# Loading q for the next two blocks in small pieces from two queues, and moving half of a block's inner sums behind a later product

## The chip, the cores and the metric

The kernel runs on one core of a Trainium2 chip. A core has five engines that work side by side: TensorE (PE in the profile, with its weight loads shown apart as PEld), VectorE (DVE), ScalarE (ACT), GpSimd (POOL) and SyncE (SP), which here only starts DMA transfers. TensorE writes to PSUM; VectorE and ScalarE read PSUM and free it for the next product. Each engine works through its own instructions in order. The metric is the device time of one execution in microseconds (us); lower is better.

## The reference

Inputs are q, k, v of shape (8, 8, 576, 64) (batch, heads, sequence, head size), a gain of 64, and three weight matrices. All is float32.

```python
kv  = einsum('bhsd,bhse->bhde', k, v)
out = einsum('bhsd,bhde->bhse', q, kv)
rms = sqrt(mean(out * out, axis=-1, keepdims=True) + 1e-06)
x   = (out / rms * g_norm).transpose(0, 2, 1, 3).reshape(4608, 512)
g   = x @ w_gate                       # 512 x 1536
silu = g / (1 + exp(-g))
result = (silu * (x @ w_val)) @ w_out  # 1536 x 512
```

## The kernel before

**Blocks.** The 4608 rows of x are worked on in nine blocks of 512 rows. Block n needs the products kv of the batches that its rows belong to, its q, and from these its x (class `Att`). Then the block goes through a feed-forward stage (class `Ffn`) of two halves: `up`, which makes h = silu(x w_gate) * (x w_val), and `down`, which multiplies h by w_out. Blocks 0, 1 and 2 run alone, blocks 3 to 8 in pairs (class `Pair`).

**Fast products.** The matrix products use a scheme of seven products in place of eight (P1 to P7), with sums of operands made beforehand and sums of results made afterwards. From block 2 on it is used twice, one level inside the other. The outer sums of x are made by `sums`, and the inner sums (four operations over 128 x 896 elements, lines 132 and 133) by `inner_sums`. The sums of results are additions on VectorE that read PSUM (`r<-b,r`, `r<-c,r`, `r<-a,r` on line 132), and copies on ScalarE (line 803). PSUM has three banks named b, two named c, one named a and two named m; a product can start only when its bank has been emptied.

**Block 2's up** (class `Inner`) has twelve units: three groups d, each with four sets g of outer products. A unit runs seven inner products. Its weights are not resident: 128 x 512 pieces ("leaves", `t<-w`, lines 922 and 925) stream from DRAM into a pool of nine tiles. `Stream.pump`, called after each product, issues the next load as soon as the tile nine places back is free; all these loads stand on SP's queue.

**Work placed between.** While block 2's up runs, the attention work of block 3 and part of block 4's is placed in it. `up` takes a table `fill`: the entry i runs when the i-th unit's products have been issued. `ahead` makes this table: visits that make kv on TensorE (line 344), loads of k and v (line 294), loads of q (line 312), the transposes of block 3's q on VectorE (line 360), q times kv (line 399), squares on ScalarE (line 412), the reciprocal root in nine small VectorE steps (lines 442 to 444), the scaling (line 134) and the turning of x (line 459). Steps on VectorE are put into a list `chores`, and one is taken from it behind each product.

**q.** For a block, q is loaded in two tiles (i = 0, 1) of 128 x 1024. `load_quarters` fills a tile with 16 transfers (24 to 40 KB each for blocks 3 and 4: 32 partitions, runs of 128 bytes), eight for each half. In `ahead` a call moves eight of them, all on SP's queue, at one place: entries 1, 2, 3 and 4 for block 3, entries 6, 7, 8 and 9 for block 4.

**The order.** A planner orders each engine's instructions by its own estimate of when each can run; the order in the program is a priority and not a command. `tc.issue_after(x)` makes instructions on x's engine come behind x. Every DMA transfer, from whichever queue, is given one of eight completion semaphores in turn, and it waits until the transfer eight places before it in the planner's order has landed.

**Down.** `Down` runs P1, P6, P5, P7, P2, P4, P3. Behind P1 come the next block's products of q and kv and the rest of its attention (`steps`). The `then` table of `down` lets the caller place more: for block 2, `{1: blocks[PAIRED].inner_sums}` places the four inner sums of block 3 behind P1.

Of the kernel before, what the change touches and what calls it, by code (L numbers as in the profile page):

```python
# [18 lines left out]
def kernel(  # L19
# [41 lines left out]
    nc = tc.nc  # L61
# [152 lines left out]
    class Att:  # L214
# [83 lines left out]

        def load_quarters(self, i, pairs=(0, 1)):


            if pairs[0] == 0:
                self.q.append(ld_pool.tile([P, LD], F32, name="ld")[:, 0 : 2 * BLK])
            to = self.q[i].rearrange("p (j g d) -> p j g d", j=2, d=P // 4)
            cut = 2 * self.n
            spans = [(self.n - 1, S - D * self.n, 0, cut), (self.n, 0, cut, BLK // 32)]
            for j in pairs:
                for r in range(4):
                    h, d = divmod(r, 2)
                    for b, s0, g0, g1 in spans:  # L310
                        if g1 > g0:
                            nc.sync.dma_start(
                                out=to[32 * r : 32 * (r + 1), j, g0:g1],
                                in_=q[b, 4 * i + 2 * j + h, s0 : s0 + 32 * (g1 - g0), 32 * d : 32 * (d + 1)].rearrange(
                                    "(g p) d -> p g d", p=32
                                ),
                            )

        def load_q(self, i):
            if self.quarters:  # L320
# [132 lines left out]
        def turn_x(self, i):  # L453
            xt = self.xts[:, i].rearrange("p t j u d -> p t j (u d)")
            for j in range(0, NS, 2):
                ps = m_psum.tile([P, 2, 2, P], F32, name="m")
                for e in range(2):
                    for t in range(2):
                        self.turned_x = nc.tensor.transpose(ps[:, e, t], xt[:, t, j + e], ident)
                self.copied = nc.scalar.activation(  # L460
                    out=self.x[:, 2 * i + j // 2], in_=ps.rearrange("p e t c -> p e (t c)"), func=ACT.Copy, scale=gain
                )
# [51 lines left out]
        def half(self, i, pools=None):  # L514
            self.product(i, pools)
            self.root(i)
            self.scale(i)
            self.halves.append(self.scaled)
# [553 lines left out]
    class Ffn:  # L1072
        def __init__(self, n, att):
            self.n, self.att = n, att
            self.h = h_alone if n < PAIRED else h_slots[(n - PAIRED) % 2]
            self.ps, self.leaf_room, self.ended, self.owed = {}, None, None, None

            self.making, self.later, self.latest = [], [], []
            self.chores = []
            self.visited = None  # L1080

        def store(self, o, t, columns=slice(None)):
# [17 lines left out]
        def up(self, fill):  # L1100

            self.s1 = s_pool.tile([P, NP, HB], F32, name="s1")
            units = []
            for d in range(NP // 2):
                if self.n < DEEP:
                    units += [Up(self, 2 * d), Up(self, 2 * d + 1)]
                else:
                    shared = {}
                    units += [Inner(self, d, g, shared) for g in range(4)]
            units[0].prepare()  # L1110
            last = None
            for i, this in enumerate(units):
                if i + 1 < len(units):
                    units[i + 1].prepare()
                for unit, p in this.sequence(last):
                    if unit:
                        visited, self.visited = self.visited, None
                        with tc.issue_after(visited.ins) if visited else ExitStack():
                            unit.multiply(p)
                        self.make(4)  # L1120
                        if self.chores:
                            self.chores.pop(0)()
                last = this
                fill.get(12 * (i + 1) // len(units), lambda: None)()
            self.down_ = Down(self)
            self.down_.turn_t(5)
            for unit, p in last.sequence(None):
                if unit is None:
                    last.multiply(p)
# [136 lines left out]

    def ahead(ffn, att, then):

        def visits():
            visit(ffn, att, (0, 1))  # L1270
            att.load_quarters(0, (0,))

        def second():
            att.load_quarters(0, (1,))
            then.load_kv(0)

        def turn():
            visit(ffn, then, (0,), True)
            then.load_kv(1)
            ffn.chores += [lambda i=i: att.turn_q(i) for i in range(2)]  # L1280

        def half(i):
            with tc.issue_after(ffn.multiplied.ins):
                att.heads(i, range(NS), (m_psum, m_psum))
            ffn.visited = att.multiplied
            ffn.chores += att.chores(i)
            then.load_quarters(i, (0,))

        def turn_x(i):
            with tc.issue_after(ffn.multiplied.ins):  # L1290
                att.turn_x(i)
            ffn.visited = att.turned_x
            if i == 1:
                ffn.chores += att.sum_steps()

        def last():
            visit(ffn, then, (1,), True)
            while owed_sends:
                owed_sends.pop(0)()

        att.homes = {
            "qt": h_alone[:, 8:12], "sq": span(0, 8).rearrange("p (f t) -> p f t", f=4),
            "xts": span(8, 8).rearrange("p (f t) -> p f t", f=4),
        }

        def again(i):
            then.load_quarters(i, (1,))

        return {
            1: visits, 2: second, 3: lambda: att.load_quarters(1, (0,)), 4: lambda: att.load_quarters(1, (1,)),  # L1310
            5: turn, 6: lambda: half(0), 7: lambda: again(0), 8: lambda: half(1),
            9: lambda: (turn_x(0), again(1)), 10: lambda: turn_x(1), 11: last,
        }

    for n in range(PAIRED):
        ffn = Ffn(n, blocks[n])
        nxt = blocks[n + 1]
        if n == 0:

            with tc.issue_after(squared.ins), tc.issue_after(scaled.ins):  # L1320
                weights(2)
            ffn.plain_up(0, (0,))
            copied = blocks[0].copied
            blocks[0].turn_x(1)
            for f in range(NF):
                with tc.issue_after(blocks[0].copied.ins if f else copied.ins):
                    weights(2 * (f + 2))
                ffn.plain_up(f) if f else ffn.plain_up(0, (1,))
            weights(len(pieces))
            pairs = wo.rearrange("p (j e) d -> p e j d", e=2)  # L1330
            t2(pairs[:, 0, :, HD:DM], pairs[:, 1, :, HD:DM], pairs[:, 0, :, 0:HD])
            nxt.room = xi_alone.rearrange("p a b c -> p (a b c)")

            with tc.issue_after(sent.ins):
                for i in range(2):
                    nxt.load_kv(i)
                for i in range(2):
                    nxt.load_q(i)
            ffn.plain_end()
            for g in range(2):  # L1340
                nxt.kv(g)
            nxt.turn()
        elif n == 1:

            def third():
                visit(ffn, nxt, (0,))
                nxt.load_kv(1)

            def two_thirds():
                visit(ffn, nxt, (1,))  # L1350
                for i in range(2):
                    nxt.load_q(i)

            ffn.up({4: third, 8: two_thirds})
            nxt.turn()
            blocks[PAIRED].load_kv(0)
        else:
            ffn.up(ahead(ffn, nxt, blocks[PAIRED + 1]))
            nxt = blocks[PAIRED + 1]
            nxt.turn()  # L1360
            for g in range(2):
                blocks[PAIRED + 2].load_kv(g)
        if n:
            ffn.down_.opens = n + 1
        ffn.down(nxt, {1: blocks[PAIRED].inner_sums} if n == 2 else {})
        if n == 1:
            blocks[PAIRED].load_kv(1)
        if n == 0:
            blocks[2].load_kv(0)

            with tc.issue_after(nxt.halves[0].ins):
                for j in range(NP // 2):
                    t2(wv[j][:, 0:2], wv[j][:, 2:4], wg[j][:, 0:2])
            with tc.issue_after(ffn.down_.s4.ins):
                for j in range(NP // 2, NP):
                    t2(wv[j][:, 0:2], wv[j][:, 2:4], wg[j][:, 0:2])
# [60 lines left out]
```

## Time and profile before

| | us |
|---|---|
| median of 7 runs (1031.59 to 1036.12) | 1033.76 |
| profiled execution | 1034.03 |
| its span, first to last instruction | 1032.3 |
| TensorE busy | 1000.4 (97%) |
| VectorE busy | 684.7 (66%) |
| GpSimd busy | 360.6 (35%) |
| ScalarE busy | 228.9 (22%) |
| block 2's up, TensorE's first to last product in it | 270.9 to 371.8 |
| mean granted TensorE clock | 0.993 |

In the profile a line such as `L132 DVE TENSOR_TENSOR r<-b,r` is the instruction's line in the kernel, its engine, its operation and its output and inputs by the program's names. In a timeline the first number is the start and the second the length of the merged group in microseconds, `xN` the number of instructions; in brackets at the end stands how long the engine stood idle before it and what it waited for. `SPq` rows are DMA transfers being issued by SP; the data lands some microseconds later. In tables of stretches each engine has its busy time and, in brackets, its instructions; behind them come the granted TensorE clock as a share of full speed, the mean busy share of the 16 DMA engines and GB/s.

### The profile page before, as it was taken

The page shows a single profiled execution, that of the slowest core. Times are in us where ns is not written, and L with a number is a line of the kernel's source. Part 1 is how long each engine was busy: PE and PEld are TensorE (multiplying, and loading weights), DVE is VectorE, ACT ScalarE, POOL GpSimd, SP SyncE. Part 2 cuts the span into 40 slices and gives each one's busy share as a digit, 9 for nine tenths or more (in the row PEclk, how much of TensorE's full clock was granted, in tenths as well). Part 3 has the DMA queues.
Part 4 walks back from the last instruction along what each step waited for, and adds up shares of the span by engine and source line. Part 5 has one row for each costly group of instructions (what it writes and reads, how often), then busy time and mean ns, then how long its engine had stood idle before and what let it go on. Part 6 is the DMA issues. An engine that isn't in the chain of part 4 may idle for free.

```text
span 1032.3 us, 17746 instructions
## 1 busy us (share of the span) xinstructions
PE 1000.4 (97%) x6774; PEld 844.2 (82%) x6774; DVE 684.7 (66%) x1166; ACT 228.9 (22%) x357; POOL 360.6 (35%) x283
## 2 busy tenths in 40 slices
PE   6999999999989799999999999999999999999998
PEld 4544688888988788888888888888888888888887
DVE  2998788888557884665667656566676566666211
ACT  2765112221211211112111211211212112121100
POOL 0000263534024631345555102465652025556600
PEclk9999999999989989999999999999999999999999
DMA  8689543768888846586742454667403545543011
GB/s 230 203 254 266 116 86 128 238 204 206 246 196 201 239 110 160 150 217 170 171 133 62 114 127 146 164 167 186 126 12 72 117 151 163 153 142 106 1 41 41
DMA packets 255637, 155.20 MB, mean 150 GB/s; under 512 B 141632, under 2 KB 234816, under 8 KB 255552
## 3 DMA queue, kind: packets, MB, share of 16 engines
q1 hardware_dynamic: 224832, 150.13, 53.1%
q10 hardware_dynamic: 30656, 3.94, 2.4%
q8 instruction: 54, 0.88, 0.4%
q14 instruction: 31, 0.25, 0.1%
q0 software_dynamic: 64, 0.00, 0.0%
HBM read 117.97 MB, written 28.70 MB: 142 GB/s over the span
## 4 chain that ended last, share of the span: by engine, by line
PE 71%; DMA 4%; SPq 1%; DVE 0%; issue 0%; ACT 0%; DVEq 0%; ACTq 0%
PE b L789 24%; PE b L621 16%; PE c L789 11%; PE c L621 8%; PE a L789 6%; PE a L621 4%; DMA t<-w 2%; PE m L399 1%; PE m L344 1%; DMA w<-arena 1%; DMA ld<-in_q_dram 1%; DMA ld<-in_v_dram 1%; DVE r L132 0%; SPq L294 0%; SPq L962 0%
## 5 line engine op out<-in xcount | busy, mean ns | idle before, releaser
L789 PE MATMUL b<-arena,t 128*128 128x256 f32 (+1 forms) x1248 | 281.6, 365 | 13.4 <-DVE r L132 8.0
L789 PEld LDWEIGHTS b<-arena,t 128*128 128x128 f32 x1248 | 222.6, 193 | 44.9 <-DVE r L132 12.0
L132 POOL TENSOR_TENSOR r<-r 128x256 f32<-128x256 f32 (+1 forms) x105 | 110.5, 1054 | 310.8 <-DMA t<-w 153.0
L132 DVE TENSOR_TENSOR r<-b,r 128x512 f32<-128x512 f32 (+1 forms) x273 | 162.3, 607 | 85.6 <-PE b L789 78.8
L132 DVE TENSOR_TENSOR r<-c,r 128x512 f32<-128x512 f32 (+1 forms) x179 | 109.2, 618 | 94.9 <-PE c L789 45.0
L789 PE MATMUL c<-arena,t 128*128 128x256 f32 (+1 forms) x624 | 140.5, 362 | 0.9 <-ACT r L803 0.7
L133 POOL TENSOR_TENSOR t<-wo 128x512 f32<-128x512 f32 x54 | 78.4, 1474 | 173.9 <-DVE wo L132 105.5
L132 DVE TENSOR_TENSOR r<-a,r 128x512 f32<-128x512 f32 (+1 forms) x99 | 62.5, 632 | 105.0 <-PE a L621 66.8
L134 POOL TENSOR_TENSOR arena<-r 128x1024 f32<-128x1024 f32 (+1 forms) x46 | 96.2, 2107 | 95.7 <-DVE r L132 78.7
L789 PEld LDWEIGHTS c<-arena,t 128*128 128x128 f32 x624 | 111.8, 192 | 14.5 <-ACT r L803 1.1
L133 DVE TENSOR_TENSOR arena<-arena 128x512 f32<-128x512 f32 (+3 forms) x101 | 102.5, 1027 | 19.1 <-PE b L621 11.9
L621 PE MATMUL b<-wo,arena 128*128 128x256 f32 x432 | 99.1, 382 | 0.8 <-POOL arena L134 0.8
L621 PE MATMUL b<-t,arena 128*128 128x256 f32 x432 | 96.3, 380 | 0.0
L621 PEld LDWEIGHTS b<-wo,arena 128*128 128x128 f32 x432 | 81.1, 190 | 13.3 <-DVE arena L134 1.3
L621 PEld LDWEIGHTS b<-t,arena 128*128 128x128 f32 x432 | 82.1, 190 | 11.4 <-issue 0.2
L803 ACT COPY r<-b 128x512 f32<-128x512 f32 x63 | 36.9, 585 | 222.2 <-PE b L789 211.0
L789 PE MATMUL a<-arena,t 128*128 128x256 f32 (+1 forms) x288 | 72.3, 369 | 0.0
L789 PEld LDWEIGHTS a<-arena,t 128*128 128x128 f32 x288 | 53.2, 193 | 6.4
L621 PE MATMUL a<-wo,arena 128*128 128x256 f32 x216 | 48.4, 379 | 0.0
L621 PE MATMUL c<-t,s 128*128 128x256 f32 x216 | 48.1, 379 | 0.0
L621 PE MATMUL c<-wo,arena 128*128 128x256 f32 x216 | 48.1, 379 | 0.0
L621 PEld LDWEIGHTS c<-wo,arena 128*128 128x128 f32 x216 | 41.1, 190 | 5.5
(118 smaller groups left out, 1116.9 us busy)
## 6 DMA issues: line engine op xcount, KB each, us to landing
t<-w SPq DMA_DIRECT2D x219, 256.0 KB, 3.3
t<-w SPq DMA_DIRECT2D x75, 128.0 KB, 3.5
out_dram<-r SPq DMA_DIRECT2D x17, 512.0 KB, 3.0
ld<-in_k_dram SPq DMA_DIRECT2D x26, 288.0 KB, 5.2
ld<-in_v_dram SPq DMA_DIRECT2D x26, 288.0 KB, 6.1
ld<-in_moe_w_gate_dram SPq DMA_DIRECT2D x12, 512.0 KB, 4.8
ld<-in_moe_w_val_dram SPq DMA_DIRECT2D x12, 512.0 KB, 4.7
ld<-in_moe_w_out_dram SPq DMA_DIRECT2D x12, 512.0 KB, 5.5
```

The source lines that it names most:

```text
L132: add = lambda e, o, a, b: e.tensor_tensor(out=o, in0=a, in1=b, op=OP.add)
L133: sub = lambda e, o, a, b: e.tensor_tensor(out=o, in0=a, in1=b, op=OP.subtract)
L134: mul = lambda e, o, a, b: e.tensor_tensor(out=o, in0=a, in1=b, op=OP.mult)
L344: self.positions = nc.tensor.matmul(self.kv_ps[r][u * D : (u + 1) * D, g, :], lhsT=k[:, u, c, :], rhs=v[:, u, c, :], start=(c == 0), stop= ...
L399: self.multiplied = nc.tensor.matmul(self.ps[i][u][p : p + D, t, j, :], lhsT=self.qt[rows, 2 * i + t, j, p : p + D], rhs=kvs[b % 3][rows, ...
L621: self.ffn.multiplied = nc.tensor.matmul(banks[e][:, e], lhsT=lhsT, rhs=rhs, start=first and i == 0 and (e == 0 or banks[0] is not banks[1 ...
L789: self.ffn.multiplied = nc.tensor.matmul(to, lhsT=weight, rhs=self.operand(o, p), start=begins, stop=True, skip_group_check=True,)
L803: nc.scalar.copy(out=dst, in_=ps)
```

## The change

Three things change, all in or right behind block 2's up.

1. `load_quarters` is now made of single steps (`quarter_steps`), one for each transfer, and the steps can go to several queues in turn. `ahead` puts all 16 steps of a tile into a list `sends`, with SP and ScalarE taking turns, and `up` takes two steps from the list behind each product.
2. The tiles are asked for at other places: block 3's at entries 1 and 2 in place of 1 to 4, block 4's at entries 6 and 8 in place of 6 to 9.
3. The four inner sums of block 3 are placed behind P5 of block 2's down in place of P1.

```diff
         def load_quarters(self, i, pairs=(0, 1)):
+            for step in self.quarter_steps(i, pairs, (nc.sync,)):
+                step()
+
+        def quarter_steps(self, i, pairs, queues):
...
+            parts = [(j, r, *part) for j in pairs for r in range(4) for part in spans if part[3] > part[2]]
+            return [
+                lambda queue=queues[k % len(queues)], part=part: load(queue, *part) for k, part in enumerate(parts)
+            ]
...
                         if self.chores:
                             self.chores.pop(0)()
+                        for _ in range(2):
+                            if self.sends:
+                                self.sends.pop(0)()
...
     def ahead(ffn, att, then):
 
+        def load(att, i, *pairs):
+            ffn.sends += att.quarter_steps(i, pairs, (nc.sync, nc.scalar))
+
         def visits():
             visit(ffn, att, (0, 1))
-            att.load_quarters(0, (0,))
+            load(att, 0, 0, 1)
 
         def second():
-            att.load_quarters(0, (1,))
+            load(att, 1, 0, 1)
             then.load_kv(0)
...
-            then.load_quarters(i, (0,))
...
-        def again(i):
-            then.load_quarters(i, (1,))
-
         return {
-            1: visits, 2: second, 3: lambda: att.load_quarters(1, (0,)), 4: lambda: att.load_quarters(1, (1,)),
-            5: turn, 6: lambda: half(0), 7: lambda: again(0), 8: lambda: half(1),
-            9: lambda: (turn_x(0), again(1)), 10: lambda: turn_x(1), 11: last,
+            1: visits, 2: second, 5: turn, 6: lambda: (half(0), load(then, 0, 0, 1)),
+            8: lambda: (half(1), load(then, 1, 0, 1)), 9: lambda: turn_x(0), 10: lambda: turn_x(1), 11: last,
         }
...
-        ffn.down(nxt, {1: blocks[PAIRED].inner_sums} if n == 2 else {})
+
+        def inner_sums():
+            with tc.issue_after(ffn.multiplied.ins):
+                blocks[PAIRED].inner_sums()
+
+        ffn.down(nxt, {5: inner_sums} if n == 2 else {})
```

In the planner's order this moves 32 of the 64 q transfers of blocks 3 and 4 from SP's queue to ScalarE's. Of the four inner sums, two stay where they were among VectorE's instructions, and two now stand behind the additions of the last unit.

## The prediction

> **What bounds the kernel now.** I read the page first: TensorE (PE) is busy for 97% of the span, so time can only come from places where PE stands still or runs at a lower granted clock.
>
> ```profile
> PE 1000.4 (97%) x6774; PEld 844.2 (82%) x6774; DVE 684.7 (66%) x1166; ACT 228.9 (22%) x357; POOL 360.6 (35%) x283
> PEclk9999999999989989999999999999999999999999
> ```
>
> Then the table of stretches of 10 us over block 2's up (271 to 369 us); its columns are the stretch, its length, the busy time of PE, PEld, DVE, ACT, POOL, the granted clock, the DMA share and GB/s.
>
> ```profile
> 290.00:300.00 10.00, 7.09 (x61) 6.76 (x60) 6.51 (x11) 1.06 (x1) 3.09 (x2) 0.95 0.85 192
> 300.00:310.00 10.00, 8.93 (x54) 8.77 (x55) 2.67 (x4) 2.81 (x4) 2.15 (x1) 0.71 0.79 193
> 350.00:360.00 10.00, 7.25 (x120) 6.49 (x118) 9.63 (x13) 2.15 (x5) 5.91 (x5) 1.00 0.93 295
> 360.00:370.00 10.00, 6.42 (x39) 6.37 (x40) 8.47 (x11) 0.00 (x0) 4.00 (x2) 0.66 0.89 255
> ```
>
> PE loses time and clock here, and from 370 us on it is full again. Third, PE's waits in order of time name what was late; there are six (also 1.07 and 0.62 us for t at 309.32 and 323.36, and 1.71 us for VectorE at 327.87):
>
> ```profile
> 299.73 2.93 PE L789 MATMUL b<-arena,t 128*128 128x128 f32 x12 [2.91 <-DMA t<-w]
> 340.58 0.71 PE L789 MATMUL a<-arena 128*128 128x128 f32 x4 [1.51 <-DVE r L132]
> 363.58 1.22 PE L789 MATMUL b<-arena,t 128*128 128x128 f32 x4 [6.26 <-DVE r L132]
> ```
>
> Microsecond stretches show the clock at 0.50 from 299 to 305.8 and from 363 to 367.1, after the waits of 2.91 and 6.26 us; after 1.71 and 1.51 us it stayed at 1.00. Half clock costs half the time: 6.1/2 = 3.1 and 3.5/2 = 1.8 us. So six stalls and two slow stretches make 19 us in all. Last, the queues behind the two long ones: SP's, then VectorE's and GpSimd's.
>
> ```profile
> 283.42 0.91 SPq L922 DMA_DIRECT2D t<-w  x2
> 285.92 5.28 SPq L312 DMA_DIRECT2D ld<-in_q_dram  x8
> 291.25 1.27 SPq L294 DMA_DIRECT2D ld<-in_k_dram  x2
> 293.95 1.56 SPq L922 DMA_DIRECT2D t<-w  x3
> ```
> ```profile
> 355.15 1.24 DVE L132 TENSOR_TENSOR arena<-arena 128x896 f32<-128x896 f32 x1
> 356.31 6.28 DVE L133 TENSOR_TENSOR arena<-arena 128x896 f32<-128x896 f32 x3
> 362.51 1.01 DVE L132 TENSOR_TENSOR r<-b,r 128x256 f32<-128x256 f32 x2
> ```
> ```profile
> 355.39 6.25 POOL L133 TENSOR_TENSOR t<-wo 128x512 f32<-128x512 f32 x3
> ```
>
> The first stall's weights were issued at 293.95, behind eight q and four k/v transfers, and landed at 299.6. The second is VectorE's: four inner sums stand ahead of the adds that free PE's bank, three of them at 2.09 us beside GpSimd's three at 2.08.
>
> **The change, part by part.** No transfer, matmul or VectorE operation is added or removed; they move.
>
> *Inner sums.* In the built order two of the four still stand where they were, two go behind the transposes of q and the last unit's adds. The first two end at 355.15 + 1.2 + 2.1 = 358.4, the add that PE waits for at 359.05 instead of 363.5. PE then waits 1.75 us, close to the 1.71 that left the clock alone: 4.5 + 1.8 = 6.3 us won. The moved two now lie ahead of the products that make h (L134). Walking VectorE on from 359.05: two adds (0.95), a transpose (1.2), three adds (1.55), a transpose (1.2), two adds (1.2), a sum (1.2), an add (0.6), a sum (1.2), the first product (1.2) end at 369.3. PE, which needed 8.6 us at full clock from restart to the last third of P1 (363.58 to 373.97 less 1.8), and now does 0.7 us of block 3's heads before it, arrives at 368.3 and waits 1.0 to 1.2. P1 and the heads end at 372.4 instead of 377.99: **-5.6 us**. Bounds: -6.3 (nothing given back) and -2.0 (the residual wait halves the clock after all, 1.8, and the moved sums also take 2.09 each, 1.8).
>
> *VectorE's small steps of the root.* Before, nine steps of 0.17 and a scaling of 1.29 ran in a row (324.35 to 326.8) ahead of the adds that PE waited 1.71 us for. In the new order those steps alternate with adds, and of the second root's two scalings one goes behind the adds. The rows bound it by 0 and 1.71 + 1.51 = 3.2; I take **-1.8**: 1.2 of the first wait, since one scaling still stands ahead of the adds, and 0.6, one add, of the second.
>
> *The q transfers.* 64 of them (0.44 us to issue, 0.31 to 1.42; 3.2 us to land, 1.7 to 6.4) stood on SP in groups of eight. Now 32 go to ScalarE's queue, one per queue behind each product, and block 3's 32 come in the first two and a half units rather than four. What they cost ScalarE, 32 x 0.44 to 0.97 (its eight at 389.20 took 7.73 us), is 14 to 31 us in a stage of 100 us where it is busy for 18; the cover is its idle time, and it is gone only where it is waited for. Two couplings come in. ScalarE is in order, so a transfer behind its SiLU goes when the SiLU has run. And the planner hands the transfers of both queues eight completion semaphores in turn: each waits until the one eight places ahead has landed (the "q waits for t" of the SP queue, 16 waits, 7.9 us in this stage). So SP can wait for a transfer that ScalarE has not issued.
>
> That happens at the first stall. Before, 12 transfers stood between the last weight piece at 285.45 and 293.95. Now 18 do, 11 on SP and 7 on ScalarE, and SP's first weight piece waits for the fourth q behind the SiLU, which waits for VectorE and ran at 290.51 for 1.06 us: 291.6 + 3 x 0.44 + 3.2 to land = 296.1, 2.2 us later than before. The other end comes from the eight in flight: from the first q at 276.9 on 35 transfers stand ahead of this piece, before 25; with the 5.5 us that the first q's took to land, 25/8 x 5.5 = 17.2 gives 294.1, near the 293.95 seen, and 35/8 x 5.5 = 24.1 gives 301.0, 7.0 later. I take 5, a little above the middle, since the count fits the row of before and the DMA engines are between 0.73 and 1.04 busy here. The next five pieces, at 302.83 before, have no q left ahead of them but ScalarE's last and go at 302 to 304 all the same; PE comes to them 5 us later, so its wait of 1.07 goes. At 323.36 the wait of 0.62 goes (block 4's q comes later), and one of the same size comes: a weight piece waits there for a ScalarE transfer behind a copy at 315.68. Sum 5 - 1.1 = **+3.9**. Ends: -7.7 (all three waits and the 3.1 of slow clock gone) and 7.0 - 1.1 = +5.9.
>
> With one queue, SP took 5.2 to 6.4 us to issue eight q, and from 276 to 283 us the DMA engines were 0.95 busy, but from 283 to 296 only 0.54 to 0.74: the rows leave room for a second queue there. [...]
>
> **Sum.** -5.6 - 1.8 + 3.9 = -3.5. The profiled execution took 1034.03 us (span 1032.3 and 1.7 around it), 0.27 above the median of the seven runs, 1033.76; I take the difference off the median: **1030.3 us**. PE is full after 370 us, so what is won there reaches the end.
>
> **The rivals.**
> - *Weights arrive in time.* Had the first piece gone out by 290.9 (296.6 less the 5.65 it took to land), the DMA stalls vanish: -5.6 - 1.8 - 7.7 = -15.1, 1018.7 us. For it: SP has one q fewer ahead of it and its own share of the issue time is halved. Against it: the wait for the SiLU.
> - *Given back.* Sums at -3.0, roots at -1.0, q at +4: no change, 1033.8. For it: VectorE is 9.63 and 8.47 of 10 busy in 350 to 370, so two sums moved by a few us may only move the wait. Against: the walk above finds gaps.
> - *Slower: SP waits for ScalarE.* Price: 7.0 at the first stall, of which nothing is recovered if the next pieces slip as well, and up to 2.6 more near 321, where a weight piece that went at 317.0 waits for ScalarE's q behind its copy: -7.4 + 9.6 = +2.2, 1036.0 us. It decides where the lateness of SP's pieces adds up to 7.4 + 2.1 = 9.5 us. For it: the count of 25 transfers fits a landing of 5.5. Against it: q landed in 3.2 us in the median.
> - *That the sums don't move* can be ruled out: the built order shows two of them behind the adds.
>
> **How the numbers follow.** Likeliest 0.54 (own range 1025 to 1031.6), weights in time 0.11, given back 0.14, slower 0.21. A measurement of this kernel tells about 0.2%, 2.1 us, from no change. Faster 0.54 + 0.11 = 0.65, same 0.14, slower 0.21. The range leaves out most of the first rival and the tip of the last: 1023.5 to 1036.5. The bounds of all three terms together would be -17.2 and -2.0 + 5.9 = +3.9, 1016.6 to 1037.7.
>
> **What would show it.** Right: the wait near 363 falls to 1.5 to 2.5 us with the clock at 1.00 behind it; a short wait for L134 in P1; the wait of 2.91 us near 299.7 grows to 5 to 10, its t issued at 296 to 301 behind ScalarE's q; SP rows that wait for ScalarE's q. Wrong: that wait gone; ScalarE's copies late enough to stop PE; VectorE standing at the transpose of block 3's second q; the wait for VectorE at 357 still over 3 us.

## The result, and the profile after

The changed kernel takes 1029.6 us (median of 18 runs, 1027.28 to 1034.2), the kernel before, measured with it, 1035.02 us. The ratio is 0.996 with a 95% interval of 0.9949 to 0.9971, so it is 4.1 us faster (3.0 to 5.3); 3.5 were forecast. The means, 1030.48 and 1034.62, lie 4.1 us apart as well; the medians lie 5.4 apart, since single runs of one kernel spread over 7 to 8 us. The profiled execution took 1029.29 us with a span of 1027.5, 4.8 us below the span before.

The first line of the page of the changed kernel:

```profile
PE 999.5 (97%) x6774; PEld 842.4 (82%) x6774; DVE 684.6 (67%) x1166; ACT 228.9 (22%) x357; POOL 360.7 (35%) x283
```

Every engine has as many instructions as before, and its busy time differs by 1.8 us at most; what changed is where TensorE stands. The stretches of 10 us (busy time of PE, PEld, DVE, ACT, POOL, then granted clock, DMA share and GB/s), changed kernel:

```profile
290.00:300.00 10.00, 6.26 (x57) 6.07 (x55) 5.41 (x10) 1.06 (x1) 3.08 (x2) 1.00 0.95 163
300.00:310.00 10.00, 7.33 (x42) 7.33 (x43) 2.98 (x4) 1.76 (x3) 0.00 (x0) 0.66 0.92 249
330.00:340.00 10.00, 8.59 (x110) 8.12 (x111) 7.88 (x17) 2.66 (x5) 2.34 (x1) 0.83 0.88 228
350.00:360.00 10.00, 8.69 (x135) 8.14 (x133) 9.48 (x14) 2.54 (x5) 7.33 (x7) 1.00 0.77 259
360.00:370.00 10.00, 8.97 (x85) 8.28 (x89) 9.85 (x15) 1.06 (x1) 3.87 (x2) 1.00 1.05 246
```

From 350 to 370 us TensorE now works 17.66 us in place of 13.67, with the clock at 1.00. From 290 to 310 it works less than before (13.59 against 16.02), and there is a new slow stretch between 330 and 340. TensorE's waits in order of time say the same; all those over 0.3 us in block 2's up and in P1 are here:

```profile
302.67 2.97 PE L797 MATMUL b<-arena,t 128*128 128x128 f32 x12 [6.40 <-DMA t<-w]
311.73 1.13 PE L797 MATMUL b<-arena,t 128*128 128x128 f32 x8 [0.83 <-DMA t<-w]
331.29 2.02 PE L797 MATMUL b<-arena,t 128*128 128x128 f32 x8 [1.68 <-DMA t<-w]
361.03 0.71 PE L797 MATMUL b<-arena,t 128*128 128x128 f32 x4 [2.35 <-DVE r L132]
370.91 1.99 PE L629 MATMUL b<-wo,arena 128*128 128x256 f32 x8 [0.40 <-DVE arena L134]
```

The wait of 6.26 us is down to 2.35. The first wait for weights has grown from 2.91 to 6.40, one of 1.68 is new, and the two waits for VectorE at 327.87 and 340.58 are gone. SP's queue behind the first two waits, changed kernel:

```profile
287.98 1.44 SPq L315 DMA_DIRECT2D ld<-in_q_dram  x3
289.47 1.26 SPq L294 DMA_DIRECT2D ld<-in_k_dram  x2
290.82 1.25 SPq L294 DMA_DIRECT2D ld<-in_v_dram  x2
293.60 5.09 SPq L315 DMA_DIRECT2D ld<-in_q_dram  x4
299.02 1.41 SPq L930 DMA_DIRECT2D t<-w  x3
...
301.50 2.82 SPq L315 DMA_DIRECT2D ld<-in_q_dram  x5
304.42 1.42 SPq L930 DMA_DIRECT2D t<-w  x3
```

The first weight piece goes at 299.02, 5.07 us later than before, and the next ones behind five more q at 304.42 (302.83 before). VectorE behind the long wait (the moved sums are the last two of 128 x 896):

```profile
356.71 2.13 DVE L132 TENSOR_TENSOR arena<-arena 128x896 f32<-128x896 f32 x1
358.77 1.60 DVE L133 TENSOR_TENSOR arena<-arena 128x896 f32<-128x896 f32 x1
...
366.81 1.07 DVE L133 TENSOR_TENSOR arena<-arena 128x896 f32<-128x896 f32 x1
...
368.64 1.08 DVE L133 TENSOR_TENSOR arena<-arena 128x896 f32<-128x896 f32 x1
369.64 2.35 DVE L134 TENSOR_TENSOR arena<-r 128x1024 f32<-128x1024 f32 x2
```

**Which edit moved the sums.** The built orders, that is each engine's instructions as the planner puts them out, show something that the diff hides. The edit of the inner sums by itself moves no instruction on any engine: the kernel before with that edit alone has the order of the kernel before, and the changed kernel without it has the order of the changed kernel. So the whole change is the q edit, and the gain on the sums is a by-product of the planner's new order. e2 agrees: it has the third edit, but q on one queue, and its sums stand where they stood before. To have the sums alone, their place had to be forced.

### The profile page after: what moved, and what is told of

The parts are those of the page before. It is cut to its first block, busy times and chain, and to the rows that moved or that the text cites. A ratio compares the mean times of both kernels' runs of the same rounds, so it can differ in the third digit from the quotient of the medians.

```text
span 1027.5 us, 17747 instructions
## 1 busy us (share of the span) xinstructions
PE 999.5 (97%) x6774; PEld 842.4 (82%) x6774; DVE 684.6 (67%) x1166; ACT 228.9 (22%) x357; POOL 360.7 (35%) x283
## 3 DMA queue, kind: packets, MB, share of 16 engines
q10 hardware_dynamic: 40384, 5.12, 3.2%
## 4 chain that ended last, share of the span: by engine, by line
PE 73%; DMA 2%; DVE 1%; issue 0%; ACT 0%; ACTq 0%; DVEq 0%; SPq 0%
PE b L797 25%; PE b L629 16%; PE c L797 12%; PE c L629 8%; PE a L797 6%; PE a L629 4%; DMA t<-w 2%; PE m L352 1%; PE m L407 1%; DMA ld<-in_q_dram 1%; DVE r L132 0%; PE m L467 0%; PE b L407 0%; DVE arena L134 0%; PE a L407 0%
## 5 line engine op out<-in xcount | busy, mean ns | idle before, releaser
L134 POOL TENSOR_TENSOR arena<-r 128x1024 f32<-128x1024 f32 (+1 forms) x46 | 96.2, 2108 | 100.6 <-DVE r L132 80.8
L133 DVE TENSOR_TENSOR arena<-arena 128x512 f32<-128x512 f32 (+3 forms) x101 | 100.2, 1004 | 19.1 <-PE b L629 11.9
L629 PEld LDWEIGHTS c<-t,s 128*128 128x128 f32 x216 | 41.0, 190 | 5.6
```

What stands on the lines that cost most here:

```text
L133: sub = lambda e, o, a, b: e.tensor_tensor(out=o, in0=a, in1=b, op=OP.subtract)
L134: mul = lambda e, o, a, b: e.tensor_tensor(out=o, in0=a, in1=b, op=OP.mult)
L629: self.ffn.multiplied = nc.tensor.matmul(banks[e][:, e], lhsT=lhsT, rhs=rhs, start=first and i == 0 and (e == 0 or banks[0] is not banks[1 ...
```

## The experiments

Ratios are to the kernel before, run with each group on the same chip (medians 1033.55, 1033.63 and 1033.57 us in the three groups); with an interval of 95%.

### e1: the sums alone

```diff
-                add(nc.vector, dst, ps, dst)
+                added.append(add(nc.vector, dst, ps, dst))
...
-        ffn.down(nxt, {1: blocks[PAIRED].inner_sums} if n == 2 else {})
+        def inner_sums():
+            steps = list(blocks[PAIRED].inner_sums())
+            for step in steps[:2]:
+                step()
+            for step, a in zip(steps[2:], (-3, -1)):
+                with tc.issue_after(added[a].ins):
+                    step()
+
+        ffn.down(nxt, {1: inner_sums} if n == 2 else {})
```

> The kernel before, with one thing moved: the third and fourth inner sums of block 3 are put on VectorE behind the last unit's additions, as they stand in the changed kernel. q is loaded as before. (In the built order the edit of the inner sums by itself moves nothing; the sums moved because the planner saw other times for q. So this is the way to have that move alone.) My theory, the term of -5.6 us: the wait of 6.26 us near 363 falls to 1.5 to 2.5 us with the clock at 1.00, the first DMA stall near 299.7 stays at about 2.9 us, and the kernel takes 5 to 7 us less than before, a ratio of 0.993 to 0.995. Rival 'given back': the wait only moves to the products that make h, and not more than 2 us are won (0.998 or above). Rival that the gain is the q loading's: the same time as before.

Measured: 1028.17 us, ratio 0.9942 (0.9927 to 0.9956), 6.0 us less. TensorE's two long waits, kernel with the sums alone:

```profile
300.02 2.76 PE L789 MATMUL b<-arena,t 128*128 128x128 f32 x12 [3.31 <-DMA t<-w]
359.85 0.71 PE L789 MATMUL b<-arena,t 128*128 128x128 f32 x4 [2.13 <-DVE r L132]
```

The long wait is 2.13 us, the clock from 350 to 370 is 1.00, and the first DMA wait is much as before (3.31 against 2.91). The move of two sums alone gives at least as much as the whole change: 0.9942 against 0.996, though the intervals overlap a little. So "given back" falls, and so does the rival that the gain is q's.

### e2: early q on SP's queue alone

```diff
-            ffn.sends += att.quarter_steps(i, pairs, (nc.sync, nc.scalar))
+            ffn.sends += att.quarter_steps(i, pairs, (nc.sync,))
```

> The changed kernel with all q transfers left on SP's queue (two behind each product, block 3's asked for as early as in the changed kernel). The planner then leaves the four inner sums where they were, so this is the early q alone. If the number of transfers ahead of the first weight piece of the stall is what counts (18 in place of 12, eight in flight, 0.67 us each in the row of before): the piece goes at 297.5 to 299, TensorE waits 6 to 8 us near 300, and the kernel takes 1 to 4 us more than before (ratio 1.001 to 1.004). If it is ScalarE's queue (its transfers behind the SiLU, which SP's piece waits for): without it the piece goes at 294 to 295.5 as before, the wait is 3 to 4 us, and with the root steps spread the kernel takes 0 to 2 us less than before (0.998 to 1.000). The wait of over 6 us near 363 is there in both.

Measured: 1035.77 us, ratio 1.0016 (1.0007 to 1.0026), 1.7 us more. SP and TensorE, kernel with SP's queue alone:

```profile
285.37 3.45 SPq L315 DMA_DIRECT2D ld<-in_q_dram  x6
...
297.08 1.41 SPq L930 DMA_DIRECT2D t<-w  x3
```
```profile
300.15 3.18 PE L797 MATMUL b<-arena,t 128*128 128x128 f32 x12 [4.12 <-DMA t<-w]
365.54 1.23 PE L797 MATMUL b<-arena,t 128*128 128x128 f32 x4 [6.27 <-DVE r L132]
```

Without ScalarE's queue the piece still goes 3.1 us later than before. The count theory had 297.5 to 299, the ScalarE theory 294 to 295.5; 297.08 is outside both and close to the first. TensorE's wait, 4.12, is smaller than the count theory said (6 to 8): it went on 3.07 us after the piece was issued, where it took 5.78 before. The wait of 6.27 at the sums is back, as it should be.

### e3: two queues, q at the old places

```diff
-            1: visits, 2: second, 5: turn, 6: lambda: (half(0), load(then, 0, 0, 1)),
-            8: lambda: (half(1), load(then, 1, 0, 1)), 9: lambda: turn_x(0), 10: lambda: turn_x(1), 11: last,
+            1: visits, 2: second, 3: lambda: load(att, 1, 0), 4: lambda: load(att, 1, 1), 5: turn,
+            6: lambda: (half(0), load(then, 0, 0)), 7: lambda: load(then, 0, 1),
+            8: lambda: (half(1), load(then, 1, 0)), 9: lambda: (turn_x(0), load(then, 1, 1)), 10: lambda: turn_x(1), 11: last,
```

(`visits` and `second` each load one half of tile 0.)

> The changed kernel with q asked for at the places of before (entries 1 to 4 and 6 to 9), but still two behind each product and half from ScalarE's queue. The sums stand where the changed kernel has them. The first weight piece of the stall has about 14 transfers ahead of it in place of 18, but it still waits for a q transfer that ScalarE issues behind its SiLU (the second behind it, in place of the fourth). Count theory: the piece goes at 295 to 296, TensorE waits 3.5 to 4.5 us there, 2 to 2.5 us less than in the changed kernel: 1026.5 to 1028 us. ScalarE theory: SiLU ends at 291.1, two transfers at 1.2 us each and 3.5 to 4 us to land: 297 to 298, a wait of 5 to 5.5 us, and 1028 to 1029 us.

Measured: 1028.52 us, ratio 0.9949 (0.9937 to 0.9961). The piece went at 297.58 and TensorE waited 4.59 us. The time of the piece and that of the kernel are those of the ScalarE theory, the wait is nearer the count theory's. By itself this run would speak for ScalarE; the issue times of all kernels, lined up below, do not.

### e4: all four sums behind the last additions

As e1, on the changed kernel, with `zip(steps, (-3, -2, -1, -1))`.

> The changed kernel with all four inner sums of block 3 on VectorE behind the last unit's additions, two of them behind the products that make h. The wait of 2.35 us near 361 is VectorE's first two sums (2.1 and 1.6 us); without them TensorE should not wait there. If the path then runs through the last unit's additions alone, 1.5 to 2.4 us are won over the changed kernel (1027.5 to 1028). Rival: VectorE is full here, so what is won at 361 is waited for again at the last third of P1 (for the sums of h, which come later) or at block 3's heads, and the time is within 1 us of the changed kernel's.

Measured: 1029.28 us, ratio 0.9952 (0.9939 to 0.9965). TensorE no longer waits near 361, and no wait of that length takes its place up to P6. Against the changed kernel (0.996) that is 0.8 us less, within the intervals, so the forecast gain of 1.5 to 2.4 us is not shown; the rival, that the time stays within 1 us, fits. e8 does the same on q of before.

### e5 and e6: q on GpSimd's queue

```diff
-            ffn.sends += att.quarter_steps(i, pairs, (nc.sync, nc.scalar))
+            ffn.sends += att.quarter_steps(i, pairs, (nc.sync, nc.gpsimd))
```

and for e6 `(nc.gpsimd,)`.

> The changed kernel with the second half of the q transfers on GpSimd's queue in place of ScalarE's. GpSimd's transfers have completion semaphores of their own, so SP's weight pieces no longer wait for a transfer of the other queue; the number of q transfers, their sizes and the places where they are asked for stay. The order of VectorE's inner sums stays nearly as in the changed kernel. If that wait of SP is what made the stall longer: the first piece goes at 291 to 294.5 in place of 299.0, TensorE waits 3.5 us or less in place of 6.4, and the kernel takes 2 to 5 us less than the changed one (1025 to 1028). [...]

> The changed kernel with all q transfers of blocks 3 and 4 on GpSimd's queue. SP then has only four k/v transfers ahead of the first weight piece, whose place is free from 287.9: it goes at 288 to 290.5, TensorE does not wait near 300 and its clock stays at 1.00 there (6.4 us of wait and 3 us of slow clock gone): 1019 to 1023 us if nothing takes their place. Rival: q arrives late, 32 transfers in one queue; VectorE stands at the transposes of q (299 and 306 us in the changed kernel) and TensorE behind it, or GpSimd's sums are late: 1027 us and above.

Measured: e5 1026.14 us, ratio 0.9921 (0.9898 to 0.9945); e6 1030.06 us, ratio 0.9964 (0.9948 to 0.998). SP and TensorE in e5:

```profile
289.19 2.04 SPq L315 DMA_DIRECT2D ld<-in_q_dram  x4
291.33 2.05 SPq L930 DMA_DIRECT2D t<-w  x3
```
```profile
296.30 0.71 PE L797 MATMUL b<-arena,t 128*128 128x128 f32 x4 [0.55 <-DMA t<-w]
297.57 0.71 PE L797 MATMUL b<-arena,t 128*128 128x128 f32 x4 [0.56 <-DMA t<-w]
298.89 0.71 PE L797 MATMUL b<-arena,t 128*128 128x128 f32 x4 [0.60 <-DMA t<-w]
```

The piece goes 7.7 us earlier than in the changed kernel, the wait of 6.40 us becomes three of 0.55 to 0.60, and the clock stays at 1.00 from 290 to 310; the piece, the wait and the time all lie where the expectation had them. The same 32 transfers hardly hold up the weights when they stand on GpSimd's queue. That queue has a round of eight semaphores of its own (102 to 109 in the trace of e5). SP's and ScalarE's transfers of the changed kernel go through 100, 101 and 110 to 115, and GpSimd's two in the kernel before already had 102 and 103. So in these kernels the round of eight is not shared by every queue, only by SP's and ScalarE's. GpSimd is busy for 18.5 us more (379.2 against 360.7), which TensorE does not wait for. In e6 the other side of the scale is reached. TensorE's two long waits, VectorE's wait and a stretch of e6:

```profile
299.13 2.45 PE L797 MATMUL b<-arena,t 128*128 128x128 f32 x12 [4.52 <-DVE r L132]
342.96 1.11 PE L467 MATMUL m<-ident,arena 128*128 128x128 f32 x4 [6.36 <-DVE arena L134]
```
```profile
297.25 1.25 DVE L368 STREAM_TRANSPOSE arena<-ld 128x1024 f32<-128x1024 f32 x1 [4.66 <-DMA ld<-in_q_dram]
```
```profile
330.00:340.00 10.00, 6.60 (x59) 6.41 (x57) 9.58 (x15) 2.79 (x5) 9.98 (x13) 1.00 0.66 170
```

No wait for weights is left, but q is late: VectorE stood 4.66 us at the first transpose (297.25), and TensorE stands behind VectorE. From 330 to 340 GpSimd is busy for 9.98 of 10 us; each of the 32 transfers of e5 costs it 0.58 us (18.5 / 32). The rival of e6 was right.

### e7: k and v later

On e1: `then.load_kv(0)` moves from entry 2 to entry 3, ahead of the q there.

> As the kernel with the sums alone moved (q as before, SP only), and the four k and v transfers of block 4 are asked for one unit later (entry 3 in place of 2). Eight transfers stand ahead of the first weight piece in place of twelve. If their number sets when it goes: 291.3 to 291.8 in place of 294.2 and the wait near 300 falls from 3.3 to under 1 us, with no slow clock behind it; the pieces that went at 303.0 go up to 2.6 us later, and the wait of 1.8 us for them grows to 3 to 4.5. Net 1 to 4 us less than the sums alone: 1024 to 1027 us. Rival: the later wait takes all of it, clock and all: 1028 us or above.

Measured: 1027.79 us, ratio 0.9942 (0.9922 to 0.9962), the same as e1. Kernel with k and v later:

```profile
290.81 1.43 SPq L922 DMA_DIRECT2D t<-w  x3
```
```profile
306.55 0.92 PE L789 MATMUL a<-arena,t 128*128 128x128 f32 x4 [4.85 <-DMA t<-w]
```

The piece went 3.4 us earlier with four transfers fewer ahead, and the wait near 300 is gone. But the next pieces, which now have the four k and v ahead of them besides eight q, went no earlier (302.92 against 303.01 in e1), and TensorE, which comes to them sooner, waits 4.85 us, with a slow stretch behind it (0.50 from 307 to 310). The rival had the mechanism and nearly the time (1028 us or above): with q, k and v all on SP's queue the lateness only moved.

### e8: all four sums, q of before

As e1, on the kernel before, with `zip(steps, (-3, -2, -1, -1))`.

> The kernel before with all four inner sums of block 3 on VectorE behind the last unit's additions; q as before. Against the kernel with two sums moved, the wait of 2.13 us near 360 should go, as in the changed kernel with four sums moved, where the run was about 1 us faster than with two: 1026 to 1028 us. Against that one it tells the price of the q part again: 1 to 3 us less than it. Rival: no difference to two sums moved, since VectorE is full from 350 to 380 (1028 to 1029).

Measured: 1026.77 us, ratio 0.9924 (0.9907 to 0.994). That is 1.9 us less than e1, but the intervals overlap. The wait near 360 is gone, as expected.

### e9, e10, e12: both steps together

e9 is e5 with all four sums as in e4. e10 asks for block 3's second q tile at entry 3 in place of 2; e12 asks for q at the places of e3.

> The changed kernel with the second half of the q transfers on GpSimd's queue and all four inner sums of block 3 behind the last unit's additions: the two steps that each were faster than the changed kernel, together. If their gains add: the wait of 2.35 us near 354 and the slow clock behind it (3.4 us at half speed) go, 2 to 3.5 us less than with GpSimd's queue alone: 1022.5 to 1024.5 us. Rival: VectorE is full there, as it was with q of before and four sums (1.4 us gained over two sums), or GpSimd's sums beside VectorE's take the rest: 1025 to 1026.5 us.

> The same, with block 3's second q tile asked for one unit later (entry 3 in place of 2). SP then has eight transfers ahead of the first weight piece, and GpSimd none of the second tile: the piece goes at 289 to 290.5 in place of 291.3 and the three short waits near 297 (1.7 us in all) go; the next pieces have four more q ahead of them and may be waited for. Between 1.5 us less and the same as the run with entry 2. Rival: the transposes of q on VectorE come later and TensorE waits for VectorE near 306: 1 to 3 us more.

> As the first of this group, with q asked for at the places of before (entries 1 to 4 and 6 to 9, two behind each product, half on GpSimd's queue). SP has eight transfers ahead of the first weight piece. If asking early is what costs, this is the fastest: 1021.5 to 1024 us. If the early request costs nothing once the second queue has semaphores of its own, it is within 1 us of the first of this group.

Measured: e9 1025.04 us, 0.9907 (0.9884 to 0.9929); e10 1021.02 us, 0.9872 (0.9852 to 0.9892); e12 1022.04 us, 0.9881 (0.986 to 0.9903). TensorE's waits of over 0.4 us between 290 and 370 us in e10:

```profile
298.47 0.71 PE L797 MATMUL b<-arena,t 128*128 128x128 f32 x4 [0.53 <-DMA t<-w]
300.06 0.49 PE L797 MATMUL c<-arena,t 128*128 128x128 f32 x2 [0.88 <-DMA t<-w]
318.80 0.71 PE L797 MATMUL b<-arena,t 128*128 128x128 f32 x4 [1.12 <-DVE r L132]
319.93 0.68 PE L797 MATMUL b<-arena,t 128*128 128x128 f32 x4 [0.42 <-DMA t<-w]
336.26 0.63 PE L467 MATMUL m<-ident,arena 128*128 128x128 f32 x4 [1.75 <-DVE arena L134]
```

e9 is at the edge of its rival: 1.1 us less than e5, within the intervals. e12 lies in the range that was expected if asking early is what costs, though it is not the fastest. e10 did better than expected, though its first weight piece went at 291.02, later than the 289 to 290.5 expected, and two short waits for weights stayed. e10 beats both kernels: its median is 12.6 us below the one before, and its interval lies wholly under that of the changed kernel. Asking for q later is worth 3 to 4 us by the medians of e9, e10 and e12, more than was expected of e10; the intervals of e9 and e10 overlap by a hair, those of e9 and e12 by more.

### e11: the roots alone

On e1, with every small step kept behind the addition before it:

```diff
                         if self.chores:
-                            self.chores.pop(0)()
+                            with tc.issue_after(added[-1].ins):
+                                self.chores.pop(0)()
```

> The kernel before with two inner sums moved, and in addition the small steps of the reciprocal roots and the scalings kept behind the addition of the product before (so that the second root and both pairs of scalings alternate with additions, as in the changed kernel). This is the term of -1.8 us by itself: if it is right, the waits for VectorE near 325, 328 and 341 (1.56, 0.74 and 0.75 us with the sums alone moved) fall to under 1.5 us in all and the kernel takes 1 to 2 us less than with the sums alone moved (ratio 0.9925 against 0.9942). Rival: the same additions are late by other VectorE work, as with q on SP alone, where 2.9 us of those waits stayed: no difference (0.994).

Measured: 1031.82 us, ratio 0.9987 (0.9973 to 1.0001), 4.7 us more than e1 by the ratios (3.6 by the medians). TensorE's waits in e11:

```profile
324.24 1.45 PE L789 MATMUL b<-arena,t 128*128 128x128 f32 x8 [1.13 <-DVE a L442]
327.68 0.71 PE L789 MATMUL b<-arena,t 128*128 128x128 f32 x4 [0.65 <-DVE r L132]
...
341.52 0.71 PE L789 MATMUL a<-arena 128*128 128x128 f32 x4 [1.76 <-DVE r L132]
345.38 0.94 PE L789 MATMUL b<-arena,t 128*128 128x128 f32 x6 [1.36 <-DVE r L132]
```

The three waits make 3.54 us in place of 3.05 in e1, and more come behind them. The edit also holds back the transposes of q and the outer sums, so it isn't the root steps alone: it shows that steps kept behind the additions in this way cost time, and not what the changed kernel's order of them is worth.

## Why the prediction came out right, point by point

The number was right (1030.3 forecast, 1029.6 measured), in part by luck: the errors of the terms nearly cancel. By terms, read off the same products in the two traces (before, then after):

| from, to | by the prediction | by the traces |
|---|---|---|
| start of the span to the first wait (296.82, 296.27) | 0 | -0.55 |
| to block 3's q times kv (317.36, 319.76) | +3.9 | +2.95 |
| to the kv products before P1 (354.06, 355.43) | -1.8 | -1.03 |
| to the first product of P6 (377.92, 374.26) | -5.6 | -5.03 |
| sum | -3.5 | -3.66 |

Of the 0.55 in the first row 0.49 are there when block 2's up begins (270.86 and 270.37), ahead of everything that was moved: two executions can differ by that much without the change. q came out 0.95 us better than forecast, the roots and the sums 0.77 and 0.57 worse, and that these cancel is luck. Behind P6 another 1.1 us are won up to the end of the span, 0.7 of it a wait for weights in a later block that the changed kernel does not have.

**Inner sums: right in size, wrong in what moves them.** The wait fell to 2.35 us (1.75 forecast) with the clock at 1.00, and the wait for L134 was 0.40 (1.0 to 1.2 forecast). That the clock stayed at 1.00 is luck: behind a wait of 1.91 us at the same place in e3, and of 2.35 us in e5, it was halved for 3.4 us (1.7 us lost). The prediction walked VectorE with the first two sums at 1.2 and 2.1 us, and in the changed kernel they took 2.13 and 1.60; the moved two took 1.07 and 1.08, the bound of 2.09 each did not come true. Its rows also add up to an end of P1 and the heads at 372.6 to 372.8 and not 372.4, a term of about -5.3. e1 gives this term by itself: -6.0 us (-7.5 to -4.5). The prediction listed the move as a part of its own; the built orders show that it came with the q edit, so the two terms could not be had apart by these edits.

**q transfers: right in sign and mechanism, too large by a fourth.** The piece went 5.07 us later (5 forecast), but the wait grew by only 3.5, since TensorE could go on 3.65 us after it was issued (302.67 less 299.02) and not 5.78 as before (299.73 less 293.95). The wait of 1.07 us that was to go stayed (0.83): the prediction had the next five pieces go at 302 to 304 with no q of SP's ahead of them, and five q stood there, so that they went from 304.42 on. Three pairs of runs give the price of the q edit with the roots, against the forecast of +2.1: +1.7 us (e2 and before), +1.9 (changed kernel and e1), +2.9 (e4 and e8). Only the first is measured directly, with an interval that excludes zero; the others are differences of two ratios whose intervals overlap. The step "ScalarE's SiLU holds SP's piece" and the step "eight in flight" can be told apart by lining up all kernels whose q go through this round alone. Counted from the built orders are the transfers that share the eight semaphores and stand between the weight piece before and the first piece of the wait, against the time from the first of them on SP's queue to that piece:

| kernel | transfers | us | us each |
|---|---|---|---|
| e7 | 8 | 4.77 | 0.60 |
| before | 12 | 8.03 | 0.67 |
| e1 | 12 | 7.75 | 0.65 |
| e8 | 12 | 7.24 | 0.60 |
| e11 | 12 | 7.56 | 0.63 |
| e3 (SP and ScalarE) | 14 | 9.29 | 0.66 |
| e2 | 18 | 11.71 | 0.65 |
| changed (SP and ScalarE) | 18 | 11.04 | 0.61 |
| e4 (SP and ScalarE) | 18 | 11.12 | 0.62 |

At this place the time goes with the number of transfers, whichever of the two queues they stand on. It is not constant in these traces: other groups of eight took 4.5 to 7.2 us, and in e5, e9, e10 and e12, where GpSimd's transfers run beside them, 8 to 11 took 6.8 to 8.2 us (0.68 to 0.99 each). The changed kernel's piece (299.02) is later than that of e2 (297.08), but its transfers also began later (287.98 against 285.37), so no time is left for the SiLU. ScalarE in the changed kernel:

```profile
290.02 1.06 ACT L824 ACTIVATE r<-r 128x1024 f32<-128x1024 f32 x1 [6.25 <-DVE r L132]
290.02 9.63 ACTq L315 DMA_DIRECT2D ld<-in_q_dram  x8
```

The trace agrees in detail. The piece did wait for the fourth q behind the SiLU, as the prediction said: that q had used the piece's semaphore last. But the transfers behind the SiLU did not wait for its end, as the prediction had it: the first went at 290.02, as the SiLU began (it ran to 291.08), and just after its own semaphore had come free (289.97). Behind two copies at 280.42 and 283.50 ScalarE's q went at 280.42 and 283.52, as these began. What the prediction had wrong is the landing: the fourth q was issued at 291.60 and landed at 298.95, 7.35 us later and not 3.2. So the count, 35/8 of a landing, which gave 7.0 us, was somewhat nearer to the 5.07 measured than the SiLU's end, which gave 2.2, and no gain from a second queue in the same round of semaphores is seen: with SP alone the early q cost 1.7 us, with both queues 1.9.

SP's queue with ScalarE's was thus no faster than SP's alone (the piece at 299.02 and 297.08). SP's with GpSimd's was: in e5 the same transfers on a third engine made the weight piece 7.7 us earlier and the kernel 0.4% faster than the changed one.

**The later piece.** Near 323 the prediction let one wait of 0.6 us, for a piece behind a transfer of ScalarE, replace another of its size. None of over 0.3 us came there; a wait of 1.68 us came at 331.29, with 3.4 us of half clock behind it (1.7 us lost, from the 0.83 of that stretch), and the piece issued at 327.10 that landed just before it, at 331.15, had stood behind SP's own q.

**Roots: the step that failed.** The first of the two waits for VectorE, in the kernel before:

```profile
327.87 0.71 PE L789 MATMUL b<-arena,t 128*128 128x128 f32 x4 [1.71 <-DVE r L132]
```

Both waits went, 3.2 us, but what stood in their place was that wait for weights and its slow clock. Where weights come in time (e5), VectorE is waited for again, 0.63 and 1.62 us between 320 and 330; in e2, with the early q on one queue, 2.9 us of such waits stayed (0.43, 0.96 and 1.52 from 331 to 343); and with the steps forced apart (e11) nothing is won. The -1.03 us in the table is the balance of this stretch and not a gain of the new order; how much of it the order is worth stays open, since no run moved the root steps and nothing else.

**The rivals.** "Weights in time" did not come with this change, but e5 shows that its mechanism was real: with SP's first piece at 291.33, close to the 290.9 that the prediction named, the wait of 6.40 us shrinks to three of at most 0.60. Its price was not: e5 is 4.0 us faster than the changed kernel, where this rival lay 11.6 us below the forecast, and VectorE is waited for in it (the roots, above). "Slower: SP waits for ScalarE" had the right place and half its price, 3.5 us of 7.0. "Given back" is refuted by e1.

## What to carry to other kernels

Look at the built order of each edit alone before giving it a term of the sum: here one of three edits did nothing, and its effect came from another. Where the transfers of two queues take completion semaphores from one round, count how many stand before an urgent load in that round: here that told its time (0.60 to 0.67 us each), and on which of the two queues they stood did not. Try the bulk on a queue outside the round, only as much as its engine has time to issue (half of q gained here, 1026.14 us in e5, all of it did not, 1030.06 in e6), and ask for it late (1021.02 and 1022.04 us in e10 and e12, 1025.04 in e9). When a product waits for an addition on a full engine, sums that nobody needs yet belong behind that addition (6.0 us less in e1).

## What the runs showed of the hardware that was not expected

**The clock.** A wait of 1.71 and one of 1.51 us left the granted clock at 1.00 in the kernel before, and 2.35 us did at 361 in the changed one. But 1.68 us at 331 was followed by 3.4 us at 0.50, and in e5 a wait of 2.35 us (354.35) by as much. The slow stretches came in two lengths only, 3.41 us (behind 3.31 us in e1) and 6.83 us (behind 2.91 before, and behind 6.40 after). Some began inside the wait: the one that the prediction read from 363 to 367.1 ran from 360.46 to 367.29. So the length of the wait alone does not tell what follows. At half clock TensorE ran six or seven products in a microsecond, at full clock twelve (303 to 308 and 309 to 310 us in the changed kernel), so a slow stretch that it works through costs about half its length.

The clock records of these runs tell more. In every run with more than one slow stretch they begin whole multiples of 3.4133 us apart, to within 0.002 us (61.439 us, 18 of them, in the kernel before, where the stretches began at 299.02 and 360.46; 30.719, nine of them, in the changed one, at 301.31 and 332.02), so each run can be cut into windows of that length. TensorE's busy time in a window (the first number behind the comma) goes with what follows. Two windows each of the kernel before and the changed kernel, then one of e5:

```profile
295.61:299.02 3.41, 1.21 (x11) 1.01 (x10) 1.99 (x3) 0.00 (x0) 1.68 (x1) 1.00 1.06 229
326.33:329.74 3.41, 1.87 (x16) 1.87 (x17) 2.69 (x5) 0.00 (x0) 0.00 (x0) 1.00 0.59 170
```
```profile
328.61:332.02 3.41, 1.68 (x13) 1.32 (x12) 3.01 (x8) 0.00 (x0) 1.59 (x1) 1.00 0.91 244
359.33:362.74 3.41, 1.71 (x15) 1.71 (x16) 3.41 (x5) 0.00 (x0) 2.17 (x2) 1.00 1.02 312
```
```profile
352.19:355.60 3.41, 1.25 (x11) 1.25 (x12) 3.41 (x5) 0.00 (x0) 2.63 (x2) 1.00 1.04 333
```

Half clock followed the first, the third and the last. Over all fourteen traces, between 30 and 1015 us, it followed each of the 19 full-clock windows with 1.50 us of work or less, 2 of the 18 with 1.52 to 1.90 us, and none with more. A window at half clock was followed by another when it held 2.71 us of work or less (6 of 6), and by full clock when it held 3.08 or more (21 of 21). So in these traces a wait was dear when it left 1.50 us of work or less in a window of 3.41, and where the windows fell against the wait differed from run to run. The window before a slow stretch was not always without work: the one ahead of the drop at 332.02 held 1.68 us of it.

The spread of single runs fits this. Of the 18 runs of the changed kernel the ten with a mean granted clock of 0.995 or 0.997 have a median of 1029.2 us, the eight with 0.991 to 0.993 one of 1032.25. Whether the clock is the cause, or goes with longer waits, was not tested.

**Packets.** The 32 q transfers on ScalarE's queue added 9728 packets for 1.18 MB to it (40384 against 30656), some 121 bytes each. On GpSimd's queue the same bytes are 1024 packets (1088 against 64). The queue lines of the changed kernel, then of e5:

```profile
q10 hardware_dynamic: 40384, 5.12, 3.2%
```
```profile
q0 software_dynamic: 1088, 1.18, 0.5%
```

So GpSimd's queue differs in two things at least, its own semaphores and its packets. The traces show that the wait for the other queue's transfers is gone: in the changed kernel the first piece goes (299.02) when a q on ScalarE's queue has landed (298.95), and in e5 no load on SP's queue between 270 and 305 us waits for a semaphore of GpSimd's. How much of the 7.7 us comes from that and how much from the packets, or from how the DMA engines share their time between queues, the runs don't tell.
